# Weighted sums over the values in fillings of three pairs of heads instead of two

## The chip, the cores and the metric

The kernel runs on one core of a Trainium2 chip. The metric is device time in microseconds (us). The core has the engines PE (TensorE, matmul), DVE (VectorE), ACT (ScalarE), POOL (GpSimd) and SP (SyncE, which here only issues DMAs). Each has its own in-order queue; they meet through semaphores.

## The reference

Three layers follow each other: attention with the heads mixed before and after the softmax, a mixture of eight experts with one expert per token, and a dense layer with a gate.

```python
# attention: q, k, v are (4, 12, 448, 64)
scores = scale * np.matmul(q, k.transpose(0, 1, 3, 2))
scores = np.einsum('bhij,hg->bgij', scores, w_pre)
attn = np.exp(scores - np.max(scores, axis=-1, keepdims=True))
attn = attn / (np.sum(attn, axis=-1, keepdims=True) + 1e-09)
attn = np.einsum('bhij,hg->bgij', attn, w_post)
x = np.matmul(attn, v)                       # then (1792, 768), tokens by heads*64
# experts: expert_idx and gate_w from x; w1 (8, 768, 1024), w2 (8, 1024, 768)
out[mask] = gate_w[mask, None] * (np.maximum(x[mask] @ w1[e], 0.0) @ w2[e])
# dense: w_in (768, 2048) and w_out (2048, 768) arrive as float64
h = x @ w_in
return ((h - np.tanh(h)) @ w_out).astype(np.float32)
```

## The kernel before

The attention works on 16 **tiles** T of query rows: four per batch, of 120, 120, 120 and 88 rows. Its innermost unit is a **block** of ten query rows with all twelve heads, 120 partitions; there are 180 blocks (`NBK`), twelve in a tile of 120 rows and nine in a tile of 88. The main loop (L1147) makes one **step** per block, so 180 steps and a few more to drain. In step s, PE gets, in this order:

- P(s): the mixing of heads before the softmax (L373, two records of 448 columns);
- perhaps a **filling**: scores S for a later tile (L330), or weighted sums AV for an earlier one (L430);
- T(s-2): the mixing after the softmax, which also transposes (L412, eight records of 120 columns);
- perhaps smaller fillings: transposes of q or k (L303, L287), or X, which turns the result of a tile (L464). A step with both S and AV has AV here, behind T.

DVE takes the row maximum of P(s) (`mx`, L377), then makes the matrix `w` of block s-1 (L387 to L390) from the sums of its exponentials. ACT computes the exponentials of block s from P(s) and `mx` (L380), and copies T(s-2) into `A` (L417). T(s-2) needs both `w` and `p` of its block. P has two PSUM banks, T two, and AV one (tag `d`), shared with one half of a score filling.

`side` is a dictionary from step to what is done in it besides the block. `posAV` puts AV fillings of tile T into the steps in which the blocks of tile T+1 run; `posS2` puts score fillings. Before, a tile has three AV fillings of two pairs of heads each, at p = 0, 2 and 4. A pair is eight matmuls of 64 columns of the array, two heads side by side, each in two records, so 16 records. Behind each filling ACT copies the bank to `xT` (L432). Tile 15 has its AV outside the loop, a pair at a time (L1199 to L1209).

Into the same steps go 72 of 96 **conversions** (`conv_do`) that turn pieces of the float64 weights of the dense layer into float32: three DVE operations (L117 to L119) and three POOL operations (L120 to L122) each, loaded by SP at least one step earlier, four as a rule, and stored by SP. There are four buffers for what is loaded (`craw`), two for DVE's result (`ct`) and three for what is stored (`cm`). Before, the steps of conversions are 35 with an AV filling, 29 with scores alone, and 8 of those with AV a second time.

The steps at the end also start the experts: `to_experts` in step 173 issues the first weight loads, `do1` in steps 175 and 176 converts two of them (a DVE cast, L669, and POOL subtractions). The expert stage and the dense stage follow in program order on PE.

## Time and profile before

| what | value |
|---|---|
| median of three runs | 1306.04 us (1301.5 to 1306.4) |
| profiled execution, its own time | 1305.95 us |
| its span | 1304.1 us |
| granted TensorE clock, mean | 0.998 of full speed |
| PE busy in the span | 1292.2 us (99%) |
| first and last P of the 180 steps | 19.6 and 493.0 us |

The span is the stretch from the first to the last instruction of the program; the run's time holds 1.85 us more around it. PE's records are pipelined: one is still running when the next starts, so a busy PE does not mean a PE at its peak. What a piece of work costs is read from the distance between starts.

### The profile page before, as it was taken

What the parts mean: (1) busy time and instruction counts of PE and PEld (TensorE: products, weight loads), DVE (VectorE), ACT (ScalarE), POOL (GpSimd) and SP (SyncE); (2) the same over time, 40 slices, a digit from 0 to 9 for tenths busy, and PEclk for the clock granted to TensorE, in tenths of its full rate; (3) what the DMA queues carried; (4) which work ended last, traced back from release to release, by engine and by line L of the source; (5) the groups of instructions that cost most, each with busy time, mean ns of one, the idle gap of its engine ahead of it and who ended that gap; (6) DMA issues with size and microseconds to landing.
All of it is one profiled execution on the core that took longest, in us unless ns stands there. A gap on an engine that the chain in (4) does not pass through costs nothing.

```text
span 1304.1 us, 24991 instructions
## 1 busy us (share of the span) xinstructions
PE 1292.2 (99%) x9138; PEld 1135.0 (87%) x9138; DVE 1004.9 (77%) x2179; ACT 738.5 (57%) x1502; POOL 491.3 (38%) x497
## 2 busy tenths in 40 slices
PE   8999999999999999999999999999999999999998
PEld 6777777777777778999999999999999999999998
DVE  5877877787878777777777766688888877888886
ACT  6667666666667665554444545664545446444542
POOL 1344423351444125433332223453554534445441
PEclk9999999999999999999999999999999999999999
DMA  6887665676557458778988876221212123111102
GB/s 174 265 267 213 200 201 154 190 217 187 151 180 215 158 171 301 249 261 277 268 231 215 273 235 212 89 85 49 86 49 72 50 91 113 63 49 50 49 25 87
DMA packets 153077, 210.95 MB, mean 162 GB/s; under 512 B 57686, under 2 KB 113158, under 8 KB 152950
## 3 DMA queue, kind: packets, MB, share of 16 engines
q1 hardware_dynamic: 149680, 195.37, 48.9%
q0 software_dynamic: 2480, 12.19, 2.7%
q8 instruction: 74, 1.21, 0.4%
q10 hardware_dynamic: 790, 1.74, 0.4%
q14 instruction: 53, 0.43, 0.1%
HBM read 135.71 MB, written 35.01 MB: 131 GB/s over the span
## 4 chain that ended last, share of the span: by engine, by line
PE 93%; DMA 3%; DVE 2%; ACT 1%; issue 1%; SPq 0%; DVEq 0%; ACTq 0%
PE T L412 12%; PE P L373 10%; PE AV L430 6%; PE o L1458 6%; PE o L1456 6%; PE o L1457 6%; PE h L1421 6%; PE h L1422 6%; PE h L1420 6%; PE S L330 5%; PE ypi L706 3%; PE ypi L707 3%; PE ypi L705 3%; PE hi L729 2%; PE hi L731 2%; PE hi L730 2%
## 5 line engine op out<-in xcount | busy, mean ns | idle before, releaser
L412 PEld LDWEIGHTS T<-w,p 120*112 120x112 f32 (+1 forms) x1440 | 166.2, 177 | 59.4 <-issue 46.7
L122 POOL TENSOR_TENSOR cm<-cm,ct 128x256 f32<-128x256 f32 x96 | 72.0, 750 | 315.3 <-DVE ct L119 299.7
L412 PE MATMUL T<-w,p 120*112 120x120 f32 (+1 forms) x1440 | 184.8, 271 | 0.2 <-ACT p L380 0.2
L1403 POOL TENSOR_TENSOR gl<-th,gh 128x512 fp32r<-128x512 f32 (+1 forms) x64 | 77.6, 1213 | 249.5 <-ACT gh L1402 186.5
L373 PE MATMUL P<-sr,wpre 120*120 120x448 f32 x360 | 166.3, 544 | 1.0 <-DMA sr<-ssb 1.0
L380 ACT ACTIVATE p<-P,mx 120x448 f32<-120x448 f32 x180 | 113.9, 633 | 90.2 <-DVE mx L387 76.5
L1424 ACT ACTIVATE u<-h 128x512 f32<-128x512 f32 (+1 forms) x64 | 34.9, 546 | 213.7 <-PE h L1422 213.7
L1456 PE MATMUL o<-woh,gh 128*128 128x384 f32 x448 | 151.3, 338 | 0.0
L1458 PE MATMUL o<-woh,gl 128*128 128x384 f32 x448 | 150.3, 335 | 0.0
L1457 PE MATMUL o<-wol,gh 128*128 128x384 f32 x448 | 150.0, 335 | 0.0
L1462 DVE TENSOR_TENSOR acc<-acc,o 128x384 f32<-128x384 f32 x196 | 106.4, 546 | 46.8 <-PE o L1458 45.4
L377 DVE TENSOR_REDUCE mx<-P 120x1 f32<-120x448 f32 x180 | 111.4, 619 | 29.3 <-PE P L373 27.2
L120 POOL TENSOR_TENSOR cm<-craw 128x256 f32<-128x256 f32 x96 | 65.9, 687 | 115.8 <-DMA craw<-in_moe_w_in 60.3
L417 ACT COPY A<-T 112x480 f32<-112x480 f32 x180 | 102.1, 567 | 9.8 <-PE T L412 9.7
L729 PE MATMUL hi<-xhi,w1h 128*128 128x256 f32 x336 | 95.5, 284 | 0.0
L730 PE MATMUL hi<-xli,w1h 128*128 128x256 f32 x336 | 95.3, 284 | 0.0
L731 PE MATMUL hi<-xhi,w1l 128*128 128x256 f32 x336 | 95.3, 284 | 0.0
L705 PE MATMUL ypi<-w2hi,hhi 128*128 128x384 f32 x272 | 94.1, 346 | 0.0
L430 PEld LDWEIGHTS AV<-A,v 112*64 112x64 f32 x1536 | 73.9, 137 | 21.8 <-issue 10.7
L706 PE MATMUL ypi<-w2li,hhi 128*128 128x384 f32 x272 | 91.5, 337 | 0.3 <-DVE w2li L673 0.3
L707 PE MATMUL ypi<-w2hi,hli 128*128 128x384 f32 x272 | 91.5, 336 | 0.0
L121 POOL TENSOR_SCALAR cm<-cm 128x256 f32<-128x256 f32 x96 | 87.3, 910 | 8.4
(296 smaller groups left out, 3443.7 us busy)
## 6 DMA issues: line engine op xcount, KB each, us to landing
sr<-ssb SPq DMA_DIRECT2D x176, 210.0 KB
r<-in_moe_w SPq DMA_DIRECT2D x72, 384.0 KB
r<-in_moe_w SPq DMA_DIRECT2D x52, 512.0 KB
craw<-in_moe_w_in SPq DMA_DIRECT2D x48, 256.0 KB
craw<-in_moe_w_out SPq DMA_DIRECT2D x48, 256.0 KB
wor<-wo_d SPq DMA_DIRECT2D x16, 768.0 KB
raw<-wi_d SPq DMA_DIRECT2D x15, 768.0 KB
wi_d<-cm SPq DMA_DIRECT2D x48, 128.0 KB
```

Source lines behind the costliest of these rows:

```text
L373: pe.matmul(pt[:n, :S], wpre[:n, :n], t[:n, :], start=True, stop=True)
L412: pe.matmul(pt[:CP, c * n:(c + 1) * n] if m == 10 else pv[:, c], p[:n, c * CP:(c + 1) * CP], w[:n, :] if m == 10 else wv, start=True, stop ...
L430: pe.matmul(pt[64 * hh:64 * hh + 64, x * 120:x * 120 + n], vt[b, p + x][:, hh, c, :], A[T][:, c, 2 * (p + x) + hh, :n], start=c == 0, stop ...
L705: pe.matmul(pt[:, :384], a, wh[:, n0:n0 + 384], start=f == 0, stop=False)
L706: pe.matmul(pt[:, :384], a, wl[:, n0:n0 + 384], start=False, stop=False)
L707: pe.matmul(pt[:, :384], l, wh[:, n0:n0 + 384], start=False, stop=f == KF - 1)
L729: pe.matmul(pt[:, :256], wh[:, sl], xh[:, c, :], start=c == 0, stop=False)
L730: pe.matmul(pt[:, :256], wh[:, sl], xl[:, c, :], start=False, stop=False)
L731: pe.matmul(pt[:, :256], wl[:, sl], xh[:, c, :], start=False, stop=c == KD - 1)
L1456: pe.matmul(pt[:, :384], gh[:, sl], wo[0][:, f, n0:n0 + 384], start=f == 0, stop=False)
L1457: pe.matmul(pt[:, :384], gh[:, sl], wo[1][:, f, n0:n0 + 384], start=False, stop=False)
L1458: pe.matmul(pt[:, :384], gl[:, sl], wo[0][:, f, n0:n0 + 384], start=False, stop=f == GF - 1)
```

## The change

The AV fillings of tiles 0 to 14 hold three pairs of heads instead of two, so a tile has two (p = 0 and 3) instead of three (p = 0, 2, 4), with one copy to `xT` of three pairs behind each. The bank holds 3 times 120 of 512 columns. The conversions go two each into every step with such a filling that is free for them (25 steps), and the other 22 into steps with scores and no AV, spread over the 31 that there are. Loads, buffers and everything behind the attention are as before.

```diff
-        def emit_AV2(T, p):
-            return emit_AV(T, p, act.copy, 2)
+        def emit_AV3(T, p):
+            return emit_AV(T, p, act.copy, 3)
...
         for T in range(4 * B - 1):
-            for p in range(0, NP, 2):
-                at(posAV(T, p), emit_AV2, T, p)
+            for p in range(0, NP, 3):
+                at(posAV(T, p), emit_AV3, T, p)
...
-        long_ = [k for k in free if emit_AV2 in kinds(k)]
-        mid = [k for k in free if emit_S2 in kinds(k) and emit_AV2 not in kinds(k)]
-        alone = [k for k in long_ if not {emit_X, tr_q, tr_k} & set(kinds(k))]
-        more = CA - len(long_) - len(mid)
-        steps = sorted(long_ + mid + [alone[i * len(alone) // more] for i in range(more)])
+        long_ = [k for k in free if emit_AV3 in kinds(k)]
+        mid = [k for k in free if emit_S2 in kinds(k) and emit_AV3 not in kinds(k)]
+        more = CA - 2 * len(long_)
+        steps = sorted(2 * long_ + [mid[i * len(mid) // more] for i in range(more)])
```

PE, steps 43 to 45, before (blocks of tile 3 begin in step 36; the weighted sums are those of tile 2; `ptq` is a transpose of q):

```order
L373 MATMUL P_1912<-sr_1642,wpre 120x448
L412 MATMUL T_1922<-w_1855,p_1832 112x120 x4
L373 MATMUL P_1932<-sr_1669,wpre 96x448
L412 MATMUL T_1942<-w_1919,p_1852 112x120 x4
L303 MATMUL ptq_1_1947<-ident,natq_1639 128x120 x3
L373 MATMUL P_1957<-sr_1739,wpre 120x448
L430 MATMUL AV_4_1967<-A_1235,v_4_491 64x120 x8
L430 MATMUL AV_4_1967<-A_1235,v_5_516 64x120 x8
L412 MATMUL T_2003<-w_1939,p_1916 112x120 x4
```

The same steps on PE in the changed kernel:

```order
L373 MATMUL P_1887<-sr_1627,wpre 120x448
L430 MATMUL AV_3_1896<-A_1222,v_3_463 64x120 x8
L430 MATMUL AV_3_1896<-A_1222,v_4_491 64x120 x8
L430 MATMUL AV_3_1896<-A_1222,v_5_516 64x120 x8
L412 MATMUL T_1940<-w_1848,p_1825 112x120 x4
L373 MATMUL P_1953<-sr_1654,wpre 96x448
L412 MATMUL T_1963<-w_1894,p_1845 112x120 x4
L303 MATMUL ptq_1_1968<-ident,natq_1625 128x120 x3
L373 MATMUL P_1978<-sr_1717,wpre 120x448
L412 MATMUL T_1989<-w_1960,p_1891 112x120 x4
```

The filling of pairs 4 and 5 has left step 45, the one of pairs 2 and 3 has left step 42, and one of three pairs stands in step 43.

DVE in the changed kernel from step 43 to the start of step 44 (`ct` is a conversion, `w` the matrix for T); before, step 43 has no conversion and step 45 has two:

```order
L377 TENSOR_REDUCE mx_1889<-P_1887 120x1
L387 TENSOR_SCALAR mx_1843<-mx_1843 120x1
L388 RECIPROCAL mx_1843<-mx_1843 120x1
L390 TENSOR_SCALAR w_1894<-wpost,mx_1843 120x120
L117 TENSOR_SCALAR ct_1922<-craw_1715 128x256
L118 SCALAR_TENSOR_TENSOR ct_1922<-craw_1715,ct_1922 128x256
L119 SCALAR_TENSOR_TENSOR ct_1922<-craw_1715,ct_1922 128x256
L117 TENSOR_SCALAR ct_1931<-craw_1786 128x256
L118 SCALAR_TENSOR_TENSOR ct_1931<-craw_1786,ct_1931 128x256
L119 SCALAR_TENSOR_TENSOR ct_1931<-craw_1786,ct_1931 128x256
L377 TENSOR_REDUCE mx_1955<-P_1953 96x1
```

Two conversions stand between the `w` of one step and the maximum of the next, and that maximum stands before the `w` of step 43's own block.

PE at the end of the loop, steps 177 to 181, before (weighted sums of tile 14; `X` is the first work behind the loop):

```order
L430 MATMUL AV_2_6910<-A_6407,v_2_5768 64x120 x8
L430 MATMUL AV_2_6910<-A_6407,v_3_5836 64x120 x8
L412 MATMUL T_6928<-w_6880,p_6839 112x120 x4
L373 MATMUL P_6943<-sr_6696,wpre 120x448
L412 MATMUL T_6953<-w_6903,p_6877 112x120 x4
L373 MATMUL P_6959<-sr_6720,wpre 96x448
L412 MATMUL T_6969<-w_6950,p_6900 112x120 x4
L430 MATMUL AV_4_6979<-A_6407,v_4_5915 64x120 x8
L430 MATMUL AV_4_6979<-A_6407,v_5_5989 64x120 x8
L412 MATMUL T_6996<-w_6966,p_6947 112x120 x4
L412 MATMUL T_7003<-w_6977,p_6963 112x96 x4
L464 MATMUL X_0_7027<-ien,xT_6809 120x136 x3
```

The same place in the changed kernel:

```order
L412 MATMUL T_6891<-w_6860,p_6819 112x120 x4
L373 MATMUL P_6905<-sr_6668,wpre 120x448
L430 MATMUL AV_3_6914<-A_6379,v_3_5828 64x120 x8
L430 MATMUL AV_3_6914<-A_6379,v_4_5882 64x120 x8
L430 MATMUL AV_3_6914<-A_6379,v_5_5956 64x120 x8
L412 MATMUL T_6940<-w_6883,p_6857 112x120 x4
L373 MATMUL P_6947<-sr_6692,wpre 96x448
L412 MATMUL T_6957<-w_6912,p_6880 112x120 x4
L412 MATMUL T_6967<-w_6954,p_6909 112x120 x4
L412 MATMUL T_6973<-w_6965,p_6951 112x96 x4
L464 MATMUL X_0_6997<-ien,xT_6774 120x136 x3
```

The filling that stood ahead of T in step 177 is gone, the one in step 178 is new, and the one of step 180, between the last P and the last two T, is gone.

## Rows read from the trace of the kernel before

**Rows 1.** The page: the span, and busy time and instructions by engine.

```profile
span 1304.1 us, 24991 instructions
PE 1292.2 (99%) x9138; PEld 1135.0 (87%) x9138; DVE 1004.9 (77%) x2179; ACT 738.5 (57%) x1502; POOL 491.3 (38%) x497
```

**Rows 2.** A window of the expert stage: length, PE, PEld, DVE, ACT, POOL, clock, DMA.

```profile
650.00:700.00 50.00, 47.88 (x343) 47.56 (x342) 34.89 (x68) 22.12 (x37) 11.98 (x12) 0.97 0.78 219
```

**Rows 3.** Timeline of PE, steps 60 and 61: start, length, engine, line, operation, records.

```profile
173.10 0.92 PE L373 MATMUL P<-sr,wpre 120*120 120x448 f32 x2
173.95 1.86 PE L430 MATMUL AV<-A,v 112*64 112x120 f32 x32
175.74 1.07 PE L412 MATMUL T<-w,p 120*112 120x120 f32 x8
176.65 0.92 PE L373 MATMUL P<-sr,wpre 120*120 120x448 f32 x2
177.41 0.98 PE L412 MATMUL T<-w,p 120*112 120x120 f32 x8
178.23 0.92 PE L373 MATMUL P<-sr,wpre 120*120 120x448 f32 x2
```

**Rows 4.** Timeline of PE behind the loop, weighted sums of tile 15.

```profile
498.99 2.04 PE L430 MATMUL AV<-A,v 112*64 112x88 f32 x48
500.96 0.87 PE L689 MATMUL xti<-ident,xgi 128*128 128x128 f32 x6
...
504.07 1.43 PE L430 MATMUL AV<-A,v 112*64 112x88 f32 x32
505.44 1.00 PE L464 MATMUL X<-ien,xT 128*88 128x136 f32 x6
```

**Rows 5.** Timeline of PE, step 52, weighted sums of tile 3 with 88 rows.

```profile
153.06 1.43 PE L430 MATMUL AV<-A,v 112*64 112x88 f32 x32
154.43 1.07 PE L412 MATMUL T<-w,p 120*112 120x120 f32 x8
```

**Rows 6.** Timeline of PE, step 79.

```profile
225.13 0.92 PE L373 MATMUL P<-sr,wpre 120*120 120x448 f32 x2
226.01 1.04 PE L412 MATMUL T<-w,p 120*112 120x120 f32 x8
226.89 0.55 PE L287 MATMUL ptk<-ident,natk 112*128 112x112 f32 x4
```

**Rows 7.** Timeline of PE at the end of the loop, steps 177 to 181.

```profile
487.16 0.92 PE L373 MATMUL P<-sr,wpre 120*120 120x448 f32 x2
...
489.88 1.07 PE L412 MATMUL T<-w,p 120*112 120x120 f32 x8
...
492.59 0.92 PE L373 MATMUL P<-sr,wpre 96*96 96x448 f32 x2
...
496.49 1.85 PE L412 MATMUL T<-w,p 120*112 120x120 f32 x16
498.18 0.88 PE L464 MATMUL X<-ien,xT 128*120 128x136 f32 x6
```

**Rows 8.** Timeline of DVE there: the matrices w of blocks 175 and 178.

```profile
488.76 0.28 DVE L390 TENSOR_SCALAR w<-wpost,mx 120x120 f32<-120x120 f32 x1
...
494.46 0.28 DVE L390 TENSOR_SCALAR w<-wpost,mx 120x120 f32<-120x120 f32 x1
```

**Rows 9.** Timeline of DVE, step 45: two conversions behind each other.

```profile
135.83 0.42 DVE L118 SCALAR_TENSOR_TENSOR ct<-craw,ct 128x256 int32<-128x256 int32 x1
136.29 0.43 DVE L119 SCALAR_TENSOR_TENSOR ct<-craw,ct 128x256 int32<-128x256 int32 x1
...
136.95 0.92 DVE L118 SCALAR_TENSOR_TENSOR ct<-craw,ct 128x256 int32<-128x256 int32 x1
...
137.91 0.72 DVE L119 SCALAR_TENSOR_TENSOR ct<-craw,ct 128x256 int32<-128x256 int32 x1
```

**Rows 10.** Waits of the DMA queue, 50 to 480 us: total, times, longest.

```profile
SPq L123 <- POOL cm L122: 115.4, 56, 5.4
```

More of the change, by code (lines that the diff above doesn't have):

```diff
@@ L1036, in body @@
         free = [k for k in range(12, NBK - 11) if k not in routed]
-        long_ = [k for k in free if emit_AV2 in kinds(k)]
-        mid = [k for k in free if emit_S2 in kinds(k) and emit_AV2 not in kinds(k)]
-        alone = [k for k in long_ if not {emit_X, tr_q, tr_k} & set(kinds(k))]
-        more = CA - len(long_) - len(mid)
-        steps = sorted(long_ + mid + [alone[i * len(alone) // more] for i in range(more)])
+        long_ = [k for k in free if emit_AV3 in kinds(k)]
+        mid = [k for k in free if emit_S2 in kinds(k) and emit_AV3 not in kinds(k)]
+        more = CA - 2 * len(long_)
+        print(len(long_), len(mid), more, sorted(long_), sorted(mid), sorted(routed))
+        steps = sorted(2 * long_ + [mid[i * len(mid) // more] for i in range(more)])
         for j, st in enumerate(steps):
@@ L1097, in run_fill @@
         def run_fill(fn, a):
-            tag = "d" if fn is emit_AV2 else "e"
+            tag = "d" if fn is emit_AV3 else "e"
             if fn is emit_S2:
@@ L1137, in body @@
         at_e(4, tr_en)
-        PEF = (tr_q, tr_k, emit_S, emit_S2, emit_AV2, emit_X, tr_en)
+        PEF = (tr_q, tr_k, emit_S, emit_S2, emit_AV3, emit_X, tr_en)
         for fn in [f() for f in (tr_q(1, 0, "e"), tr_q(1, 1, "d"))]:
@@ L1162, in body @@
             on = 0 <= i < NBK
-            fill.sort(key=lambda x: x[0] not in (emit_S, emit_S2, emit_AV2))
-            if fill and fill[0][0] in (emit_S, emit_S2, emit_AV2):
+            fill.sort(key=lambda x: x[0] not in (emit_S, emit_S2, emit_AV3))
+            if fill and fill[0][0] in (emit_S, emit_S2, emit_AV3):
                 run_fill(*fill.pop(0))
```

## The prediction

> **What bounds the kernel now.** First the page: PE is busy in 1292.2 of 1304.1 us, DVE 77%, ACT 57%, POOL 38% [rows 1]. The busy share of PE tells little by itself, so the second view is PE's timeline, read by the distance between starts. A step with nothing but P and T takes 178.23 - 176.65 = 1.58 us, of which P 0.76 and T 0.82 [rows 3]. That is 0.10 us for each of T's eight records, one behind the other without a hole, and most steps of the loop repeat these distances: PE is the bound in fact, and time comes only from what PE itself spends or from the few places where it waits. So I looked for what an AV filling costs PE beyond its matmuls, for the steps that are longer than others of their kind, and for what stands behind each filling that moves.
>
> **What a filling costs.** In step 60 the filling makes the step 176.65 - 173.10 = 3.55 us, 1.97 more than the plain step behind it [rows 3]. It shows in three places. The filling itself takes 1.79 from its first record to T. P before it takes 0.85 to the first AV record instead of 0.76, so 0.09 at the entry. T behind it takes 0.91 instead of 0.82, so 0.09 at the exit. The filling itself has a fixed part too: behind the loop stands one AV run of 48 records, three pairs, which takes 500.96 - 498.99 = 1.97 us, and one of 32 records, which takes 1.37 [rows 4]. The third pair cost 0.60, so two pairs are 1.20 and 0.17 is fixed. Step 52, with the same 88 rows, also shows 1.37 from AV to T [rows 5], so the fixed part is the same inside the loop. For 120 rows I take the same 0.17, which leaves (1.79 - 0.17) / 2 = 0.81 for a pair, 0.10 us for two heads side by side, eight times. A filling thus costs 0.17 + 0.09 + 0.09 = 0.35 us apart from its pairs. Bounds of this term: 0.18 if only entry and exit go (the 0.17 could be a ramp per pair that the end of the loop hides), and 0.42 if the first pair is as slow as the last.
>
> **The change, part by part.** *Fewer fillings.* The matmuls stay the same, 1536 records, and each of tiles 0 to 13 has one filling less: 14 x 0.35 = 4.9 us less. Bounds 2.5 and 5.9. Steps with scores and AV together keep entry and exit, since T stands between the two. Tile 14 is at the end of the loop and is worked out below.
>
> *Copies.* There are 15 copies fewer, of three pairs instead of two. ACT is idle for 43% of the span [rows 1], and the copy stands behind T in the step's order, so nothing on PE waits for it: 0. X of a tile comes three steps behind its last filling instead of one, which can only help. The values are loaded per pair; the reads of pairs 2 and 5 come two steps earlier than before, but still at least six steps behind the loads.
>
> *Conversions.* Their work is the same; 17 more steps hold two (25 for 8). DVE has to pass both before the next maximum. In a step with two conversions before, step 45, the second conversion's L118 takes 0.92 instead of 0.42 and its L119 0.72 instead of 0.43, while POOL works on the first one's data [rows 9]. So a doubled step costs DVE 0.79 us more than two single ones. [...] What hides it: the maximum behind the conversions must wait for its own P in any case, and after the change the step that holds two is 0.81 us longer than step 45, which PE passes without a wait now. I take 0, with 17 x 0.79 = 13.4 us as the upper bound; below nothing it cannot be worth more than the two waits of the next paragraph. In the seven score steps that lose a conversion no wait for DVE shows, so nothing comes back there. SP waits for POOL before each store, 5.4 us at most now [rows 10]; with two stores behind each other this grows by perhaps 2 us. Behind it on SP stand the relays of scores for P, which are issued seven steps ahead, over 11 us even in plain steps, and the next loads: 0. Where cover is gone, it would show as P waiting for a DMA.
>
> *Waits that go.* In step 79 P to T is 0.88 instead of 0.76 and T 0.88 instead of 0.82 [rows 6]: T waits for the matrix w of a short step, 0.18 us. Step 124 is the same place of the next batch. A three-pair filling now stands in step 78 and 123 and gives w its time: 2 x 0.18 = 0.4 less.
>
> *The end of the loop.* Tile 14 has its fillings in steps 174 and 178 instead of 174, 177 and 180. Step 174 becomes 0.81 longer. In step 177 T follows P at once, some 0.9 us after the P at 487.16, so at 488.1; but its w is ready at 488.76 + 0.28 = 489.04 [rows 7, 8], held up by the casts of `do1`. So T starts at about 489.1, a new wait of 1.0, and the next P at 489.9. Then 0.85 to the filling, 0.17 + 3 x 0.81 = 2.60 for it and 0.91 for T: last P at 494.3. Of the last three T, the second needs the w of block 178, which is ready (494.46 + 0.28) - 492.59 = 2.15 us after the start of the last P [rows 7, 8], where PE would be there after 0.76 + 0.82 = 1.58. It starts at 496.5, and X at 496.5 + 1.6 = 498.1, or 0.1 later if the last w is late. Before, X is at 498.18. So the filling that is saved here is eaten by two waits, and tile 14 costs 0.8 in all. Bounds: -0.35 if the w come as soon as wanted, +2.5 if each is a microsecond later still.
>
> *The sum:* -4.9 - 0.4 + 0.8 = -4.5 us. The stage behind is the same program, and begins earlier by this: PE bounds it but for small idle times, the largest 2.1 us in a window of 50 where weights stream in [rows 2]; their loads are issued as buffers come free, so they move along. The profiled execution took 1305.95, which is the median of the runs but for 0.1: 1306.0 - 4.5 = 1301.5 us.
>
> **The rivals.**
>
> *DVE becomes the bound in the doubled steps (slower).* Place: the 17 added steps with two conversions; price 0.79 us of DVE each [rows 9], if PE waits for all of it 13.4, so 1306.0 - 4.5 + 13.4 = 1314.9 us. It decides from 4.5 / 17 = 0.26 us a step. For it: w of the same block stands behind both conversions and the next maximum. Against it: the eight doubled steps of before have no waiting T behind them, in shorter steps. Chance 0.09.
>
> *A filling has no fixed cost worth naming.* If the entry, exit and ramp came with each pair, only waits would change: 1306.0 - 0.4 + 0.8 = 1306.4. For it: the fixed part inside the filling is a difference of two runs of one trace. Against it: entry and exit are seen twice each, 0.09. Chance 0.08.
>
> *More comes back than PE's own time.* One run of the kernel before was 1301.5, 4.5 under the others: some wait behind the attention comes and goes. If an earlier start moves the expert stage to that side, with its 2.1 us window [rows 2], the time is 1301.5 - 4.5 = 1297.0. For it: that run. Against it: the loads there follow PE. Chance 0.20.
>
> **How the numbers follow.** The forecast has 0.63, the rivals 0.09, 0.08 and 0.20. The likeliest case by itself runs from 1299.5 (the fixed cost at 0.42, no waits at the end) to 1304.5 (0.18 and waits of 2 us). The range is 1297 to 1308: below it lies half of the third rival, above it most of the first, together under 0.2. A measurement can tell 0.5%, 6.5 us, from no change, so from 1299.5 to 1312.6 is the same. Faster than that: most of the third rival and 0.05 of the forecast, 0.23. Slower: 0.07 of the first rival. The same: 0.70.
>
> **What would show it.** Right: steps with a three-pair filling and 120 rows alone at 1.58 + 0.35 + 2.43 = 4.36 us, 3.7 for 88 rows; step 79 at 0.18 less; T of step 177 waiting about 1 us and the second last T about 0.6; the last P of the loop about 4 us earlier; the same distance from X to the end. Wrong: starts of T that wait for w or p in the step two behind a doubled conversion, a maximum that begins later than 0.96 us behind its P, P waiting for a relay, or the attention shorter by 4 us and the total not.

## The result and the profile after

The changed kernel takes 1314.83 us (median of six runs, 1312.7 to 1317.7). The kernel before took 1303.77 us (median of six runs, 1301.5 to 1306.4; the prediction had 1306.04 from three of them), so the ratio is 1.0087, with a 95% interval of 1.0067 to 1.0107. The forecast was 1301.5 us, range 1297 to 1308. The change makes the kernel slower by 11 us where 4.5 us less were expected.

The page of the changed kernel, span and engines, answers to [rows 1]: PE is busy for 1.7 us more than before, and 11.3 us of span are new.

```profile
span 1315.4 us, 24993 instructions
PE 1293.9 (98%) x9138; PEld 1135.5 (86%) x9138; DVE 1019.3 (77%) x2179; ACT 738.1 (56%) x1487; POOL 490.5 (37%) x497
```

Where they lie is read from four starts on PE that both traces have: the P of step 12, the P of step 174, the first expert matmul (L746) and the first matmul of the second expert item (L729).

| stretch | before | after | difference |
|---|---|---|---|
| P of step 12 to P of step 174 | 436.7 | 440.0 | +3.3 |
| to the first expert matmul | 26.0 | 28.7 | +2.7 |
| to the second item | 37.5 | 42.8 | +5.3 |
| to the end of the span | 760.4 | 760.4 | 0.0 |

So 3.3 us are lost in the body of the attention and 8.0 at its end and just behind. That the last row is equal is partly chance: over the sixteen profiled runs of this document that stretch, whose code does not change, takes between 756.3 and 761.7 us.

**What a filling costs came out as worked out.** PE, steps 60 and 61 of the changed kernel (start, length, engine, line, operation, records), to set beside [rows 3]:

```profile
174.13 0.92 PE L373 MATMUL P<-sr,wpre 120*120 120x448 f32 x2
174.98 2.68 PE L430 MATMUL AV<-A,v 112*64 112x120 f32 x48
177.59 1.07 PE L412 MATMUL T<-w,p 120*112 120x120 f32 x8
178.50 0.92 PE L373 MATMUL P<-sr,wpre 120*120 120x448 f32 x2
```

The step takes 178.50 - 174.13 = 4.37 us, where 4.36 was forecast. Entry 0.85, filling 2.61, exit 0.91 are the terms of the sum. Over the loop a filling of three pairs adds 2.80 us to its step (2.16 with 88 rows) and one of two pairs 1.98 (1.55), so a tile of 120 rows saves 3 x 1.98 - 2 x 2.80 = 0.34 us, fourteen tiles 4.7. Step 79, too, is shorter by 0.19 us, as forecast [rows 6]; step 124, its like in the next batch, by 0.08:

```profile
229.03 0.92 PE L373 MATMUL P<-sr,wpre 120*120 120x448 f32 x2
229.79 0.98 PE L412 MATMUL T<-w,p 120*112 120x120 f32 x8
230.61 0.55 PE L287 MATMUL ptk<-ident,natk 112*128 112x112 f32 x4
```

**New waits eat it.** To find them I took each step's length less what its records cost in undisturbed steps. Steps 7 to 178 without weighted sums had 2.3 us left over before, and have 13.7 now. (Of the difference 1.2 us are not new: the score steps 35, 80 and 125 waited 0.50, 0.36 and 0.36 before too, but held weighted sums then.) The largest new ones in the body are 0.50 to 0.55 us each in the six steps 64, 68, 109, 113, 154 and 158, which hold the routing matmuls R or M; 0.4 to 0.5 in the score steps 25, 32, 77 and 122; 0.4 in 45, 90 and 135; 0.2 to 0.3 in 24, 28, 56, 101, 146, 167 and 170. Step 64 on PE; the last column is the idle time ahead and what ended it:

```profile
184.81 0.92 PE L373 MATMUL P<-sr,wpre 120*120 120x448 f32 x2
...
185.67 0.24 PE L518 MATMUL R<-ohk,ones 128*128 128x8 f16 x4
186.15 1.07 PE L412 MATMUL T<-w,p 120*112 120x120 f32 x8 [0.23 <-ACT A L417]
```

And ACT there:

```profile
185.54 0.56 ACT L417 COPY A<-T 112x480 f32<-112x480 f32 x1
```

T begins 0.05 us after the end (185.54 + 0.56) of the copy of the T before it. The code says why: R and M take their PSUM bank from T's two (`ps("c", ...)`, L512 and L541). Before, a filling stood between R and T, and the copy was over by then.

In the score steps it is `kl`, the low part of k that DVE makes. Step 25 on PE and on DVE:

```profile
77.99 0.63 PE L330 MATMUL S<-kl,qh 64*88 64x448 f32 x2
```

```profile
77.31 0.62 DVE L294 TENSOR_TENSOR kl<-ptk,kh 128x448 fp32r<-128x448 f32 x1 [0.70 <-ACT kh L293]
```

These matmuls start 0.06 us after `kl` is ready (77.31 + 0.62). Before, `kl` of this step was ready at 77.44, 1.5 us after the start of its P instead of 1.9.

**DVE.** The second and third operation of a conversion, over 50 to 480 us (busy time, then mean ns of one). Before, the means were 487 and 458. POOL works on the first piece while DVE makes the second more often, as [rows 9] show it of one step: in all 25 doubled steps the second L118 takes 0.90 to 0.93 us and the second L119 0.72.

```profile
L118 DVE SCALAR_TENSOR_TENSOR ct<-craw,ct 128x256 int32<-128x256 int32 x71 | 43.1, 606 | 2.5
L119 DVE SCALAR_TENSOR_TENSOR ct<-craw,ct 128x256 int32<-128x256 int32 x71 | 37.5, 529 | 2.4
```

SP's wait for POOL ahead of the stores, which answers to [rows 10], is hardly longer: 123.0 us in all, 5.5 at most.

**The end of the loop**, PE in steps 177 to 181, for [rows 7]:

```profile
491.36 0.92 PE L373 MATMUL P<-sr,wpre 120*120 120x448 f32 x2
492.11 0.25 PE L544 MATMUL M<-oht,p 128*128 128x8 f16 x4
494.45 1.07 PE L412 MATMUL T<-w,p 120*112 120x120 f32 x8 [2.09 <-ACT A L417]
...
499.73 0.92 PE L373 MATMUL P<-sr,wpre 96*96 96x448 f32 x2
500.48 0.98 PE L412 MATMUL T<-w,p 120*112 120x120 f32 x8
502.02 1.93 PE L412 MATMUL T<-w,p 120*112 120x120 f32 x16 [0.56 <-DVE w L390]
503.79 0.88 PE L464 MATMUL X<-ien,xT 128*120 128x136 f32 x6
```

T of step 177 starts 3.09 us behind its P; 1.94 was forecast. The last P is 7.1 us later than before, though step 174 is only 3.4 later: all of tile 14's weighted sums now stand ahead of it. DVE there, for [rows 8]:

```profile
491.89 0.69 DVE L669 CAST w1h<-r 128x1024 fp32r<-128x1024 f32 x1 [0.37 <-DMA r<-in_moe_w]
...
493.41 0.28 DVE L390 TENSOR_SCALAR w<-wpost,mx 120x120 f32<-120x120 f32 x1
...
502.53 0.28 DVE L390 TENSOR_SCALAR w<-wpost,mx 96x120 f32<-96x120 f32 x1
502.73 1.28 DVE L669 CAST w1h<-r 128x1024 fp32r<-128x1024 f32 x2
```

The last two casts of expert weights follow the last block's maximum and `w`, so they move with the last P (from 495.59 to 502.73). Behind them come POOL, with the gather of the second item's rows, and SP. POOL:

```profile
503.50 7.88 POOL L673 TENSOR_TENSOR w1l<-r,w1h 128x256 fp32r<-128x256 f32 x8 [3.31 <-DVE w1h L669]
519.14 1.24 POOL L678 DMA_INDIRECT xgi<-x_d,ids  x1 [7.77 <-DMA x_d<-raw]
```

SP:

```profile
496.12 15.61 SPq L937 DMA_DIRECT2D r<-in_moe_w  x4
511.82 0.39 SPq L474 DMA_DIRECT2D x_d<-raw  x1
```

On SP the store of tile 14's result (L474) stands behind weight loads that wait for POOL to free their buffer. PE waits for the gather, and the gather for stores of attention results. Which store comes last is told by the chain that the profile follows back (start, length, what):

```profile
513.04 5.31 DMA x_d<-raw
519.14 7.35 DMA xgi<-x_d,ids
```

It is not the one on SP. At 513.04 ACT issues the second half of tile 15's result (L472), and it lands at 518.36. By the semaphores of the trace the store of tile 14 has landed at 517.08 and the indices `ids` are ready at 516.83. Before, ACT issued the same half at 506.98, it landed at 510.54, ahead of the indices (510.77), and the gather started at 511.32. So the gather now starts 2.3 us behind its indices instead of 0.55. It also takes longer itself, 7.35 us instead of 6.0. PE:

```profile
526.63 1.02 PE L689 MATMUL xti<-ident,xgi 128*128 128x128 f32 x6 [2.78 <-DMA xgi<-x_d,ids]
...
528.62 0.52 PE L706 MATMUL ypi<-w2li,hhi 128*128 128x384 f32 x1
528.94 0.52 PE L707 MATMUL ypi<-w2hi,hli 128*128 128x384 f32 x1
```

Before, the same transposes followed at 517.59 without a wait. Behind the wait the matmuls L705 to L707 come every 0.32 us; ahead of it they came every 0.17. The windows 525 to 530 and 530 to 535 us (length; busy time and records of PE, PEld, DVE, ACT, POOL; granted clock; DMA share; GB/s) say why:

```profile
525.00:530.00 5.00, 3.37 (x16) 3.40 (x17) 1.90 (x4) 2.42 (x5) 0.01 (x1) 0.72 0.71 274
530.00:535.00 5.00, 5.00 (x24) 4.42 (x23) 4.81 (x8) 0.59 (x1) 3.46 (x3) 0.94 0.42 90
```

The granted clock is 0.72 and 0.94 of full speed. In windows of 1 us from 527 to 531 it is 0.59, 0.50, 0.50 and 0.71, with PE busy throughout. What these four windows lack to full speed, 0.41 + 0.50 + 0.50 + 0.29 = 1.7 us, is my estimate of what the fall cost. The clock fell behind an idle time of 2.78 us, and not at this place in the kernel before, which has none here. So the 5.3 us of the table's third row are about 3.0 of waiting, of which 1.8 come ahead of the gather and 1.2 lie in it, and, by this estimate, 1.7 of clock; the rest I did not trace.

The trace of the kernel before has such a fall too, later: behind a wait of 2.12 us at 685.90 its clock is 0.65, 0.50, 0.50 and 0.64 in the windows of 1 us from 687 to 691, which is 1.7 us as well by the same sum, and the changed kernel's trace has none there. Between these two spans the clock therefore cancels: it is in the third row of the table with one sign and in the fourth with the other. Over the runs it does not. The mean granted clock is 0.9978 in the six runs of the changed kernel and 0.9993 in the 71 runs of the kernel before that the experiments list, which is, by my estimate, some 2 us (0.0015 of the span).

### The profile page after: what moved, and what is told of

The parts are those of the page before. It is cut to its first block, busy times and chain, and to the rows that moved or that the text cites. A ratio compares the mean times of both kernels' runs of the same rounds, so it can differ in the third digit from the quotient of the medians.

```text
span 1315.4 us, 24993 instructions
## 1 busy us (share of the span) xinstructions
PE 1293.9 (98%) x9138; PEld 1135.5 (86%) x9138; DVE 1019.3 (77%) x2179; ACT 738.1 (56%) x1487; POOL 490.5 (37%) x497
## 4 chain that ended last, share of the span: by engine, by line
PE 81%; DVE 7%; DMA 5%; ACT 3%; issue 1%; POOL 1%; SPq 0%; POOLq 0%; DVEq 0%; ACTq 0%
PE T L412 9%; PE P L373 7%; PE o L1458 6%; PE o L1456 6%; PE o L1457 6%; PE h L1421 6%; PE h L1422 6%; PE h L1420 6%; PE AV L430 4%; PE S L330 4%; PE ypi L706 3%; PE ypi L705 3%; PE ypi L707 3%; PE hi L729 3%; PE hi L731 3%; PE hi L730 3%
## 5 line engine op out<-in xcount | busy, mean ns | idle before, releaser
L122 POOL TENSOR_TENSOR cm<-cm,ct 128x256 f32<-128x256 f32 x96 | 71.4, 744 | 287.4 <-DVE ct L119 271.4
L120 POOL TENSOR_TENSOR cm<-craw 128x256 f32<-128x256 f32 x96 | 68.6, 714 | 152.2 <-DMA craw<-in_moe_w_in 87.2
L729 PE MATMUL hi<-xhi,w1h 128*128 128x256 f32 x336 | 95.1, 283 | 0.0
L705 PE MATMUL ypi<-w2hi,hhi 128*128 128x384 f32 x272 | 94.3, 347 | 0.0
L707 PE MATMUL ypi<-w2hi,hli 128*128 128x384 f32 x272 | 91.4, 336 | 0.0
```

The costliest lines, as they stand in the source:

```text
L705: pe.matmul(pt[:, :384], a, wh[:, n0:n0 + 384], start=f == 0, stop=False)
L707: pe.matmul(pt[:, :384], l, wh[:, n0:n0 + 384], start=False, stop=f == KF - 1)
L729: pe.matmul(pt[:, :256], wh[:, sl], xh[:, c, :], start=c == 0, stop=False)
```

## Experiments

The ratios are to runs of the kernel before on the same chip; the experiments ran on several chips, so they are compared with each other by their ratios. "Body" is the distance from the P of step 12 to that of step 174: 436.7 us before, 440.0 after.

**end_180**: the changed kernel, tile 14's second filling moved behind the last P.

```diff
-                at(posAV(T, p), emit_AV3, T, p)
+                at(180 if T == 4 * B - 2 and p else posAV(T, p), emit_AV3, T, p)
```

> The changed kernel, but the second three-pair filling of tile 14 stands in step 180, between the last P and the last two T, instead of in step 178 ahead of the last P. Theory (the end of the loop costs by what hangs on the last P: its maximum, the casts of two expert weights behind that on DVE, their POOL subtractions, the weight load that waits for them on SP, the store of tile 14 behind that load, the gather behind the store, and PE): the last P comes about 2.8 us earlier, the store of tile 14 and the gather 3 to 4 us earlier, PE no longer waits 3 us for the gather, and the time falls by 4 to 6 us, to 1309 to 1311. Rival (the wait for the gather only follows from PE being late, or comes and goes by itself; most of the loss is in the steps before): less than 1.5 us comes back, above 1313.

Measured: 1311.21 us, ratio 1.0056 [1.0035, 1.0077], just above the range of the theory. The gather's transposes come 2.1 us earlier than in the changed kernel and PE does not wait for them, the second item comes 4.2 us earlier. Part of the loss hangs on the place of this filling, as the theory had it. The clock falls all the same, at another place: PE's idle time ahead of T in step 177 grows from 2.09 to 2.53 us, and behind it the granted clock is 0.57 from 494.5 to 498.5 us. Steps 177 and 178 are 3.65 and 0.78 us too long, about 1.6 of it, by my estimate from this clock, through the fall.

**conv_single**: the changed kernel, conversions spread: one in each of the 25 steps with a filling and the 31 with scores, 16 of the 25 have a second.

```diff
-        more = CA - 2 * len(long_)
...
-        steps = sorted(2 * long_ + [mid[i * len(mid) // more] for i in range(more)])
+        more = CA - len(long_) - len(mid)
+        steps = sorted(long_ + mid + [long_[i * len(long_) // more] for i in range(more)])
```

> The changed kernel, but the conversions are spread as in the kernel before: one in each free step with a three-pair filling (25), one in each step with scores alone (31), 16 of the first a second one. Theory (most of the waits that are new in the steps stand where a filling of two pairs stood and covered DVE's work: the steps with the routing, the score steps behind a transpose of k): the time changes by less than 2.5 us, and the waits of steps 64, 68, 109, 113, 154 and 158 (0.5 each) and of 25, 32, 77 and 122 (0.4 to 0.5) stay. Rival (the pairs of conversions make the waits, as the slower case of the prediction had it): 7 to 8 us come back, about 1307, and those waits are gone.

Measured: 1310.08 us, ratio 1.0055 [1.0037, 1.0073]; body 438.6, 1.35 less than after. The waits of 64, 68 and the score steps stay, so the theory holds in the body. In time more came back than the 2.5 us that it allowed. In the trace the rest lies at the end: 0.5 us up to the first expert matmul and 2.9 from there to the second item, where PE still waits 2.08 us for the gather but the clock stays at 1.00.

**pairs_before**: the kernel before with 70 of 72 conversions two by two in its 35 free steps with fillings.

```diff
-        alone = [k for k in long_ if not {emit_X, tr_q, tr_k} & set(kinds(k))]
-        more = CA - len(long_) - len(mid)
-        steps = sorted(long_ + mid + [alone[i * len(alone) // more] for i in range(more)])
+        more = CA - 2 * len(long_)
+        steps = sorted(2 * long_ + [mid[i * len(mid) // more] for i in range(more)])
```

> The kernel before with its fillings of two pairs, and 70 of the 72 conversions two each in the 35 free steps with a filling, two in steps with scores. Theory (a doubled step costs PE little; 27 added ones at 0.05 us or less): the kernel before within 2 us, about 1304 to 1306. Rival (each doubled step costs what it cost in the slower case of the prediction, 0.3 us and up to 0.79): 8 us slower and up to 21, 1312 or more.

Measured: 1315.37 us, ratio 1.0098 [1.0073, 1.0124]; body 448.0, 11.3 more than before. The theory fell. The cost does not lie on all 27 added doubled steps. Ten steps wait 0.75 to 0.82 us (24, 28, 32, 57, 73, 77, 102, 118, 122, 147), and each follows a doubled step that transposes q or k. Step 168 waits 1.1, and 44, 86, 89 and 134 0.4 each. PE, steps 23 and 24:

```profile
73.36 0.39 PE L303 MATMUL ptq<-ident,natq 88*128 88x88 f32 x3
73.59 0.94 PE L373 MATMUL P<-sr,wpre 120*120 120x448 f32 x2
74.37 0.98 PE L412 MATMUL T<-w,p 120*112 120x120 f32 x8
75.86 0.60 PE L287 MATMUL ptk<-ident,natk 112*128 112x112 f32 x4 [0.51 <-DVE ql L311]
```

DVE:

```profile
73.79 0.92 DVE L118 SCALAR_TENSOR_TENSOR ct<-craw,ct 128x256 int32<-128x256 int32 x1
74.75 0.72 DVE L119 SCALAR_TENSOR_TENSOR ct<-craw,ct 128x256 int32<-128x256 int32 x1
75.39 0.42 DVE L311 TENSOR_TENSOR ql<-ptq,qh 128x264 fp32r<-128x264 f32 x1
```

The transpose in step 24 takes the bank (tag `e`) that `ql` of step 23 has yet to read, and `ql` stands behind both conversions on DVE, of which the second is slow (0.92 and 0.72). In these ten steps the 0.79 us that the prediction had for a doubled step are all there.

**cover**: the changed kernel with conversions as in conv_single and the fillings where before they had stood as cover, at fixed places behind the first step of the next tile (tile 14's second filling is then in step 180).

```diff
-                at(posAV(T, p), emit_AV3, T, p)
+                o = (3, 9) if T == 4 * B - 2 else ((7, 11), (7, 10), (3, 9), (3, 10))[T % 4]
+                at(first[T + 1] + o[p // 3], emit_AV3, T, p)
...
```

> Two three-pair fillings in each of tiles 0 to 14, but placed by hand where PE waited in the changed kernel: in the steps with routing matmuls (7 and 11 behind the tile's end), in the steps with the transpose of k ahead of a score step (7 and 10), in the first and the tenth otherwise (3 and 9, 3 and 10), tile 14 at 3 and 9, which is step 180; conversions one each in free steps with a filling (21) and scores (35), 16 doubled. Theory (a filling's fixed cost of 0.35 us is gained for 15 fillings; the loss is cover alone): most waits go, the loop is 3 to 4 us shorter than before, the end as before: 1299 to 1302, faster than both. Rival (the cover of three fillings a tile can't be had from two, other steps wait instead): 1304 to 1309.

Measured: 1308.01 us, ratio 1.0033 [1.0020, 1.0047]; body 439.5. A miss: 1299 to 1302 was expected. Steps 64, 68 and their like have no wait now, but others have lost their filling (57, 102 and 147 wait 1.05 us each, 28, 73 and 118 0.51). This choice of two places does not cover what three covered; others were not tried.

**no_168**: the changed kernel without conversions behind step 164.

```diff
+        long_ = [k for k in long_ if k < 166]
         more = CA - 2 * len(long_)
...
```

> The changed kernel, with the two conversions of step 168 moved into score steps, so that none stands behind step 164. Theory: in the changed kernel POOL finishes its last two conversions at 473.0 and 475.6 us (before 462.2 and 465.9), SP waits for them with their stores, the last relays of scores come behind those stores, and the first weight loads of the experts behind the relays: 4.8 us behind the P of step 174 instead of 1.6. Then the loads come back to about 2 us behind that P here, the waits of steps 167 and 170 (0.5 together) go too, the first expert item starts about 3 us earlier, and the time is 3 to 4 us under the changed kernel, about 1311. Rival: the loads move, but the end of the loop is bound by DVE's casts and the gather behind it, and the time stays within 1 us of the changed kernel, 1314 to 1315.

Measured: 1314.12 us, ratio 1.0095 [1.0072, 1.0117]; body 438.9. The rival was right. The first weight loads come 5.1 us earlier, and it does not matter but for DVE's wait for them (step 177 waits 1.93 instead of 2.38):

```profile
483.19 2.78 SPq L937 DMA_DIRECT2D r<-in_moe_w  x5
```

**end_before**: no_168 with tile 14 in three fillings of two pairs, as before.

```diff
-            for p in range(0, NP, 3):
-                at(posAV(T, p), emit_AV3, T, p)
+            n = 2 if T == 4 * B - 2 else 3
+            for p in range(0, NP, n):
+                at(posAV(T, p), emit_AV3, T, p, n)
...
```

> As no_168, and the weighted sums of tile 14 in three fillings of two pairs, in steps 174, 177 and 180, as before the change. Theory: what the change costs inside the attention up to step 174 is about 3 us, and the rest of the 11 us comes from the end of the loop, which is now as before; so the time is 3 us over the kernel before, 1306 to 1308, and the shift against the kernel before is the same at step 174, at the first expert matmul and behind the first item within 1 us. Rival: the shift grows behind the loop as in the changed kernel, because the conversions of the other steps have put off SP and POOL anyway: 1310 or more.

Measured: 1308.74 us, ratio 1.0030 [1.0018, 1.0043]; the shift against before is 2.2 us at step 174, 2.2 at the first expert matmul and 3.7 at the second item. On the same chip no_168 took 5.4 us more, so tile 14 alone accounts for about half of the 11 us.

**one_tile**: the kernel before with two tiles in fillings of three pairs, tile 4 as in the changed kernel, tile 8 in the steps with R and M.

```diff
...
-            for p in range(0, NP, 2):
-                at(posAV(T, p), emit_AV2, T, p)
+            o = {4: (3, 9), 8: (7, 11)}.get(T)
+            for j, p in enumerate(range(0, NP, 3 if o else 2)):
+                at(first[T + 1] + o[j] if o else posAV(T, p), emit_AV2, T, p, 3 if o else 2)
```

> The kernel before, with two tiles alone in fillings of three pairs: tile 4 in steps 60 and 66, where the changed kernel has them, and tile 8 in steps 109 and 113, the steps with routing matmuls that before held the second and the third filling. The other tiles and, but for two or three, the conversions stand as before. Theory: a filling between a step's routing matmuls and its T is cover for ACT and DVE; tile 4 loses it, so T of steps 64 and 68 waits about 0.5 us each and the tile costs 0.7 us net (1.0 of waits less 0.35 saved); tile 8 keeps it and saves about 0.2 (0.35 less a wait of 0.15 in step 106). Rival: the waits of steps 64 and 68 in the changed kernel come from conversions that stand elsewhere there; then both tiles save 0.35 and step 64 and 68 show no wait. The time is that of before within 1 us either way.

Measured: 1307.29 us, ratio 1.0021 [1.0009, 1.0033]. Steps 64 and 68 wait 0.50 and 0.54 us; 109 and 113 do not, and 106 waits 0.15, as the theory had it. PE in step 109, where three pairs stand between R and T:

```profile
309.21 0.24 PE L518 MATMUL R<-ohk,ones 128*128 128x8 f16 x4
309.38 2.68 PE L430 MATMUL AV<-A,v 112*64 112x120 f32 x48
311.99 1.07 PE L412 MATMUL T<-w,p 120*112 120x120 f32 x8
```

The body is 1.2 us longer. Steps 89 and 134 wait 0.38 each, which I had not foreseen: there `w` (L390) takes 0.63 and 0.62 us instead of 0.28, probably beside POOL, since a few conversions had moved. The time is 3 us over the kernel before where at most 1 was expected; in the profiled run 2.4 of it lie ahead of step 0, where nothing was changed.

**tuned**: the kernel before with eight tiles in fillings of three pairs, and second conversions only in steps without transposes. The values of the next batch are loaded one step later.

```diff
...
+            o = (3, 9) if T in (0, 13) else {2: (3, 7), 3: (3, 11)}.get(T % 4) if T < 13 else None
+            for j, p in enumerate(range(0, NP, 3 if o else 2)):
+                at(first[T + 1] + o[j] if o else posAV(T, p), emit_AV2, T, p, 3 if o else 2)
...
+        long_ = [k for k in long_ if k < 166]
+        two = [15, 21, 39, 48, 60, 80, 84, 93, 105, 125, 129, 138, 150, 162]
+        steps = sorted(long_ + mid + two)
```

> The kernel before, with fillings of three pairs only where the steps that lose one did not need it: tiles 0 and 13 (offsets 3 and 9 in the next tile), 2, 6, 10 (3 and 7) and 3, 7, 11 (3 and 11); the other tiles keep three fillings of two pairs, tile 14 too. Conversions: one in each free step with weighted sums and in each score step up to 164, a second in 14 steps that make no transposes of q or k. Theory (a filling costs 0.35 us by itself; a loss of cover and a doubled conversion next to a transpose cost the rest): eight fillings saved are 2.7 us, waits of 0.5 to 1 come back, so 1.5 to 2.5 us under the kernel before, about 1301.5. Rival: the second conversions cost PE wherever they stand, 0.3 to 0.4 us each as in the run with all conversions in pairs; six more of them than before are 2 us, and the time is that of the kernel before or 1 over it.

Measured: 1304.52 us, ratio 1.0001 [0.9989, 1.0013]; body 434.8, 1.8 less than before. In the trace the theory holds; the time, for which 1.5 to 2.5 us less were expected, is the same.

**end_only**: the kernel before with tile 14 alone in two fillings.

```diff
...
-            for p in range(0, NP, 2):
-                at(posAV(T, p), emit_AV2, T, p)
+            n = 3 if T == 4 * B - 2 else 2
+            for p in range(0, NP, n):
+                at(posAV(T, p), emit_AV2, T, p, n)
```

> The kernel before with tile 14 alone in two fillings of three pairs, in steps 174 and 178, as in the changed kernel; tiles 0 to 13 and the conversions as before. Theory: the end of the loop hangs on its last P, because the maximum and the matrix w of the last block, the last two casts on DVE behind them, POOL's subtractions, the weight load behind those and the gather follow each other from there; a filling that stood behind the last P now stands ahead of it. The last P is 4 us later than before against step 174, T of step 177 waits about 2 us, the first expert item starts 5 to 6 us later, and the time is 1308 to 1311, against 1304 before. Rival: the end is late in the changed kernel because conversions and waits of the earlier steps put off DVE, POOL and SP; then with tile 14 alone the first item is within 2 us of before, and the time 1303 to 1306.

Measured: 1310.49 us (1306.05 to 1313.25), ratio 1.0040 [1.0023, 1.0058]; body as before. The distance from step 174 to the last P is 15.75 us instead of 12.44, and counted from step 174 the first expert matmul comes 2.2 us later and the second item 8.9. PE waits 2.90 us for the gather, and the clock falls for longer than in the changed kernel. Windows 520 to 525 and 525 to 530 us, columns as above:

```profile
520.00:525.00 5.00, 2.10 (x11) 1.81 (x10) 0.09 (x1) 0.48 (x1) 1.64 (x3) 0.76 1.01 368
525.00:530.00 5.00, 5.00 (x20) 4.91 (x19) 4.44 (x8) 2.53 (x4) 1.52 (x2) 0.55 0.07 28
```

The time is in the range of the theory, so the place of tile 14's fillings costs this by itself. Two things missed: the first item, expected 5 to 6 us later, and the clock, of which the theory said nothing. The store that the gather waits for last is tile 15's second half here too (issued by ACT at 509.76, landed at 515.47; tile 14's on SP at 513.82, the indices at 513.55). The profiled run is the slowest of the six, with the lowest mean clock, 0.996; the mean of the six is 0.9978.

**before_nodve and after_nodve**: both kernels without DVE's part of the 72 conversions, so the low part of these weights is missing.

```diff
...
+        if j < CONV_A:
+            t = raw[:, :, 1]
+        else:
...
-        dve.scalar_tensor_tensor(t, raw[:, :, 0], 29, t, ALU.logical_shift_right, ALU.bitwise_or)
+          dve.scalar_tensor_tensor(t, raw[:, :, 0], 29, t, ALU.logical_shift_right, ALU.bitwise_or)
```

> The kernel before, with the three DVE operations left out of the 72 conversions in the attention (POOL multiplies the upper words as they are, so the low part of the weights is missing). It is the partner of the next run. Theory: PE does not wait for DVE's conversions before the change, so the distance from the P of step 12 to that of step 174 is that of before, 436.7 us, less 0.5 to 1 for the short waits of steps 35, 79, 80, 124, 125. Rival: conversions cost PE in their steps before the change already; then it is 3 us or more shorter.

> The changed kernel with the same three DVE operations left out of the 72 conversions. In full the changed kernel takes 440.0 us from the P of step 12 to that of step 174, the kernel before 436.7. Theory (lost cover): the waits of steps 24, 25, 32, 35, 56, 64, 68, 77, 80 and their like in the later batches come from the fillings that have left, and stay, though no conversion is on DVE; only those of 28, 34, 45, 90, 135, 167, 170 go, about 1.7 us. So this run is 1 to 2.5 us longer between those two steps than its partner without the change, and the time 8 to 10 us over the partner's. Rival (DVE is the bound of the doubled steps, as the first rival of the prediction has it): without DVE's conversions the 4.9 us of fixed cost show, and the distance is 3 to 5 us shorter than the partner's.

Measured: bodies 437.5 and 437.6 us. Without conversions on DVE the change is worth +0.1 us there, not the +1 to 2.5 of the theory and far from the -3 to -5 of the rival. The partner itself missed: its body was to be 0.5 to 1 us under that of before and is 0.8 over it. Its steps 44 and 89 wait 0.55 and 0.41 us that the kernel before does not have. There `w` is late, in step 44 with 0.79 us instead of 0.28, about what it takes beside POOL in the kernel before (0.62 to 0.78):

```profile
131.15 0.79 DVE L394 TENSOR_SCALAR w<-wpost,mx 120x120 f32<-120x120 f32 x1
```

Without these two waits the change would be worth +1.1. So lost cover alone eats the 4.7 us saved: it costs 4.8 to 5.8. The waits of 64, 68, 25, 32, 77 and their like stay, and DVE's part of the conversions adds 2.2 (3.3 - 1.1) to 3.2 us (3.3 - 0.1) on top; the changed kernel with and without it differs by 2.4 (440.0 - 437.6). The times are 1308.37 us (ratio 1.0034 [1.0017, 1.0052]) and 1311.89 (1.0058 [1.0038, 1.0079]), 3.5 us apart where 8 to 10 were expected, and the partner's is 4.6 us over that of before, though its span in the profile is 1302.4. Other weights reach the later stages; I read nothing from these times.

**tuned2**: tuned, with tile 0's second filling in step 23 and only one conversion in step 21.

```diff
-            o = (3, 9) if T in (0, 13) else {2: (3, 7), 3: (3, 11)}.get(T % 4) if T < 13 else None
+            o = {0: (3, 11), 13: (3, 9)}.get(T) or ({2: (3, 7), 3: (3, 11)}.get(T % 4) if T < 13 else None)
```

> As the run with fillings of three pairs in eight chosen tiles, but the second filling of tile 0 in step 23 instead of 21, as cover for steps 24 and 25, which waited 0.28 and 0.50 there; the score step 21 keeps one conversion. Theory: those two waits go, 0.7 us less between steps 12 and 174, in all 2.5 less than before; a time of 1303 or a little under, which the runs can hardly tell from before. Rival: step 24 waits for the copies of step 23 (the same 0.3), and nothing changes.

Measured: 1302.14 us (12 runs), ratio 0.9982 [0.9970, 0.9993]; body 434.15, 2.5 less than before and 0.7 less than tuned; steps 24 and 25 have no wait over 0.1. It is the one version under the kernel before that the runs can tell from it, by 0.2%.

**r_bank**: the changed kernel, R and M in the bank of the weighted sums.

```diff
-                pp = ps("c", f"R{gi}")
+                pp = ps("d", f"R{gi}")
...
-                pm = ps("c", f"M{gi}")
+                pm = ps("d", f"M{gi}")
```

> The changed kernel, with the PSUM bank of the routing matmuls R and M (steps 64, 68, 109, 113, 154, 158, 175, 177) taken from the one of the weighted sums instead of from the two of T. Theory: R and M take one of T's two banks, so T of the same step has to wait for the copy of the T before it, some 0.4 us behind R or M; before the change a filling stood between. With the other bank the 0.50 to 0.55 us of the six steps go, 3.1 us less between steps 12 and 174 (about 436.9 against 440.0), and step 177 waits 1.3 us or so, for DVE's w alone, instead of 2.25; the time is 3 to 5 us under the changed kernel. Rival: T there waits for DVE or ACT, which the routing loads; then the six waits stay within 0.1 us.

Measured: 1312.88 us, ratio 1.0059 [1.0036, 1.0082]; body 438.1, 1.9 less than after. The six waits fall from 0.50 or more to 0.10. PE, step 64, with nothing ahead of T:

```profile
185.82 0.24 PE L518 MATMUL R<-ohk,ones 128*128 128x8 f16 x4
185.92 1.05 PE L412 MATMUL T<-w,p 120*112 120x120 f32 x8
```

So it is the bank. Some of it goes on as a wait of a later score step (70 and 115 wait 0.5 instead of 0.1), and the filling of step 178 now waits 0.68 us for `idr`, which reads M in the bank that both use. The wait of step 177 hardly changes, 2.06 instead of 2.38: T now starts with `w`, not with ACT's copy, but `w` stands behind a cast that waits 0.54 us for its load. That part of the theory missed. The time is 3.6 us under the changed kernel by the ratios, 2 by the medians.

**end_store**: end_only, and the store of tile 14 issued by ACT in two halves.

```diff
-                if T == 4 * B - 1:
+                if T >= 4 * B - 2:
                     act.dma_start(...)
```

> The kernel before with tile 14 alone in two fillings (steps 174 and 178), and the store of tile 14's result issued by ACT, half by half, instead of by SP. Theory: with the last P later the casts, POOL's subtractions and SP's next weight loads are later, and on SP the store of tile 14 is issued behind those loads (508.54 us in the run without this edit, 15.6 us of issue ahead of it); the second gather waits 8.2 us for that store, PE then 2.9 us for the gather, and works at half its clock for some us behind it. With the store on ACT the gather waits for its indices alone, the transposes come 2 us or more earlier, PE's wait falls under 1 us and the clock stays; the first matmul of the second item comes 4 to 6 us earlier than without the edit (553.1), and the time is within 3 us of the kernel before, 1304 to 1307. Rival: the gather waits for the casts and POOL's own subtractions, which stand ahead of it on POOL, and the edit gives less than 1 us.

Measured: 1308.02 us, ratio 1.0034 [1.0018, 1.0049]. Tile 14's store has landed long before the gather. The gather starts at 514.31 us instead of 516.25 in end_only, of which 0.75 is an earlier last P:

```profile
514.31 0.96 POOL L678 DMA_INDIRECT xgi<-x_d,ids  x1 [6.96 <-DVE w2li L673]
```

The operation in brackets is no input of the gather. What comes last is again tile 15's second half, issued by ACT at 509.02 and landed at 513.44, 0.6 us behind the indices; it took 4.4 us instead of 5.7. The gather takes 6.4 us instead of 7.1, and PE waits 1.07 us for it instead of 2.90. The second item comes 5.4 us earlier than in end_only, and the clock stays:

```profile
515.00:520.00 5.00, 4.79 (x24) 4.00 (x22) 3.02 (x4) 2.64 (x4) 3.98 (x5) 1.00 0.99 324
520.00:525.00 5.00, 4.13 (x27) 4.00 (x28) 2.99 (x7) 2.82 (x5) 0.17 (x1) 1.00 0.76 304
```

So the edit helps in the trace, but not by the link of the theory: the gather did not wait last for the store on SP. Why tile 15's store lands sooner without it is not shown; while it flies the DMA engines are 96% busy in the kernel before and 95% in the changed kernel, and 99% or more from 510 to 520 us in end_only. Counted from step 174, the second item still comes 4.2 us later than before. In time the gain is not shown: the intervals of end_store and end_only overlap, and the median is a microsecond over the range of the theory. The mean granted clock of its ten runs is 0.9992, against 0.9978 in end_only.

## Why the prediction was wrong

*What a filling costs* was right: 4.37 us for the step where 4.36 was forecast, 4.7 us for fourteen tiles where 4.9 was. The rival "a filling has no fixed cost" falls with it. *Waits that go* was right as far as it went, 0.19 us in step 79 and 0.08 in 124. No run shows a cost of the copies, the values or SP's stores in the loop; no_168 shows that even the late loads did not matter.

*Fewer fillings* failed by what it left out. I priced the fillings that stay and those that go, and asked only which waits a filling takes away where it arrives. I did not ask what its old step does without it. Where a three-pair filling left 64, 68 and four more, T stands bare behind R or M; r_bank and one_tile show this wait and its cause. Where it left the steps around the score fillings, PE waits for `kl`, which DVE has not made yet; that cause is read from the traces alone. By before_nodve and after_nodve, all of this costs 4.8 to 5.8 us, the whole gain and more. Step 52 and its like, which lost a filling and show no wait, are what I had in mind: most steps are like that, and some twenty are not.

*Conversions*, "I take 0", failed second: 2.2 to 3.2 us, which is 0.13 to 0.19 for each of 17 added doubled steps. The rival put 0.79 on each and decided at 0.26; so in the changed kernel its wait is there at a quarter of its price or less, and could not have turned the sign alone. That its time, 1314.9 us, is the measured one is chance. In ten steps of pairs_before, behind doubled steps that also transpose q or k, it is right in full. The sentence that the eight doubled steps of before have no waiting T behind them was true, but those eight were all chosen without transposes (`alone`); they said nothing of the others. One reading that spoke against the change held in the traces: the second conversion's L118 takes 0.90 to 0.93 us instead of 0.42 in every doubled step, the 25 of the changed kernel and the eight of the kernel before [rows 9].

*The end of the loop* failed third and is the largest, 8.0 us of 11.3 where 0.8 was forecast. Three things were missed. PE is idle for 2.1 us in step 177, not 1.0: the cast waits for its load and delays `w` by more than I took from before, and the copy on ACT, for which T waits since M has its bank, comes later still. Next, "the same distance from X to the end" took the end of PE's work for the end of the stage's work. What follows hangs on results that come behind the last P: tile 15's store, the indices, the gather. The last P moved by 7.1 us, and the gather is 2.3 us behind its indices instead of 0.55, since tile 15's store takes 5.3 us instead of 3.6. end_only shows that the place of tile 14's fillings is enough for this; what makes the store slower stays open. Last, the wait that came of it cost more than its length: behind it the granted clock fell to 0.50, 1.7 us by the estimate above; in the trace of end_store the clock stays at 1.00, though about half of the delay (4.2 of 8.9 us) is still there.

The prediction also contradicted itself here: by its own terms the last P was to come 4.9 + 0.4 - 0.8 (step 174) - (494.3 - 492.59) = 2.8 us earlier, not "about 4".

The range failed with these. Most of one rival stood above its upper end. It had no case in which several small covers go at once, nor one in which the stage behind starts later than PE's own work ends.

## What to carry to other kernels

Before a piece of work is moved, look at the step that it leaves: list which banks, copies and matrices the instruction that now stands first waits for, and when they are ready; a bound engine that shows no waits may owe that to the filling. At the end of a loop, follow the last result that other engines need, not the last instruction of the bound engine. And a doubled piece of work that costs nothing in chosen places says nothing of the places that were not chosen.

## What was not expected of the hardware

DVE's L390, a multiplication of one matrix by a column of scalars, also slows down beside POOL: the `w` of block 43 took 0.77 us in the changed kernel instead of 0.28, with POOL's L122 and L120 running from 135.93 us on, and T of step 45 waits 0.4 us for it. The kernel before has this too: in 35 steps it takes 0.62 to 0.78 us, each time with POOL's L120 running; the wait of step 79 that the prediction gave back [rows 6] came of one, of 0.70 us.

```profile
135.97 0.77 DVE L390 TENSOR_SCALAR w<-wpost,mx 120x120 f32<-120x120 f32 x1
```

And behind some waits of PE stands a stretch in which the granted clock is about half: 0.50 in windows of 1 us of the kernel before and of the changed kernel, 0.57 over 4 us in end_180, 0.55 over 5 us in end_only. The waits are 2.12 us in the kernel before, 2.53 in end_180 and 2.78 in the changed kernel, each with about 1.7 us lost by the estimate above, and 2.90 in end_only, with about 3 us lost while PE worked. Behind waits of 2.08 and 2.09 us (conv_single at 524.67, the changed kernel at 494.45) the clock stays at 1.00. No run shows by itself that the wait makes the clock fall.
